# Linear attention and FFN on one core: attention regrouped around (pk x input), 1/den spread by the matmul engine, FFN LayerNorm scale applied after the FFN, two-pass list scheduler

## Chip, cores, metric

One Trainium2 chip, one of its cores. The metric is the device time of one execution in microseconds (us), the median over repeated executions. PE is the matmul engine (TensorE), PEld its weight loads, DVE the vector engine, ACT the scalar (activation) engine, POOL GpSimd, SP the engine that issues the DMAs. "Clock" is the TensorE clock that the throttle granted, as a share of full speed.

## The reference, cut to what matters

Two linear-attention layers and two ReLU FFN layers alternate on one sequence of 2048 tokens and 512 features. There are 32 heads of 16 features, and the FFN is 1376 wide.

```python
def _A_ref(x, wqkv, wo):                       # H = 32, Dh = 16
    q, k, v = qkv[0], qkv[1], qkv[2]           # from x @ wqkv
    phi = lambda t: jnp.where(t > 0, t + 1, jnp.exp(t)) + 1e-6
    pq, pk = phi(q), phi(k)
    kv  = jnp.einsum("bhsd,bhse->bhde", pk, v)
    z   = jnp.einsum("bhsd->bhd", pk)
    num = jnp.einsum("bhqd,bhde->bhqe", pq, kv)
    den = jnp.einsum("bhqd,bhd->bhq", pq, z)[..., None] + 1e-6
    return (num / den) merged over heads @ wo
def _B_ref(x, w1, w2):
    return relu(x @ w1) @ w2

x = A_x
x = x + _A_ref(_layernorm(x), A_wqkv, A_wo)
x = x + _B_ref(_layernorm(x), B_w1, B_w2)
x = x + _A_ref(_layernorm(x), A_wqkv, A_wo)
x = x + _B_ref(_layernorm(x), B_w1, B_w2)
```

(Abridged; the last line of `_A_ref` is put in words.) Every query needs kv and z, which are sums over all tokens. So each attention has a barrier: after the last token's k and v, nothing of num or den can start before kv and z are final.

## The kernel before

The program is a list of operations with their dependences. A list scheduler simulates the engines with a fixed table of costs, emits the order of instructions on each engine and picks the PSUM banks. Tokens are tiles `i` of 128 rows, four tiles are a chunk `t`. The pieces that matter (cuts marked with `...`):

```python
# first half of an attention, per tile: k and v projections, kv accumulated with z as a 129th column
mm_group(... (psv[:, b, :],  Tb[:, i, c, :], wqkv[:, c, D:2*D],   c == 0, c == 3, False) for c in range(4) ...)
mm_group(... (psv[:, b2, :], Tb[:, i, c, :], wqkv[:, c, 2*D:3*D], c == 0, c == 3, False) for c in range(4) ...)
...          # v is evacuated to vext by ACT or DVE; phi(k): 2 operations on ACT, 2 on DVE
mms.append((kv_region(j, KVA, KVB), big[... pk ...], vext[:, i, j, 0:129], st, i == NT - 1, True))

# second half, after the barrier
# a_den: 16 matmuls of 8 columns, then + 1e-6 and a reciprocal on DVE
g.add(DVE, lambda e: e.reciprocal(rden[:, t, :], dene[:, t, :]), ...)
# a_num: 4 matmuls of 128 columns; o = num * (1/den), head by head, on DVE
g.add(DVE, lambda e: e.tensor_tensor(xn[:, i, :]..., psv[:, b, :]..., rden[...].broadcast_to([128, 32, 16]), ALU.mult), ...)
transpose_pe(i)   # chunks 0 to 2: four PE transposes and an evacuation; chunk 3: a transposing DMA
# a_wo: 4 matmuls of 512 columns, then the residual with its row sum, then the sum of squares on ACT
resid(i, b, first_layer, False, True)
ln_next(t)        # mean, variance, pow(-0.5) on POOL, -mean*rstd, normalise, transposing DMA, then the FFN
```

`phi` is evacuated in four operations: ACT x + 1, ACT exp, DVE min, DVE max. The FFN's first matmuls (`b_h`) need the transposed normalised chunk; its second (`b_out`) adds to the residual.

## Time and profile before

| | before |
|---|---|
| time, median of 3 | 308.79 us (308.68 to 308.86) |
| span of the profiled run | 307.2 us |
| PE busy / idle | 295.0 / 12.2 us |
| DVE, ACT busy | 174.7, 178.3 us |
| granted clock | 1.000 |

The first fence is from the profile's page of the kernel before. Its first line gives busy us, share of the span and instructions of each engine. The others cut the span into 40 slices; a digit is the busy share of a slice in tenths. The last line gives the shares of the chain of work that ended last.

```profile
PE 295.0 (96%) x1729; PEld 147.5 (48%) x1755; DVE 174.7 (57%) x486; ACT 178.3 (58%) x359; POOL 18.8 (6%) x29
...
PE   8999999898999999999999999989889999999996
...
DVE  5898867999830381384264556699994026030122
...
PE 81%; DVE 11%; ACT 4%; DMA 3%; issue 1%
```

PE is nearly always busy, and DVE is full over several slices in a row in only two places, 54 to 77 us and 200 to 230 us. These follow the two barriers. The next fence shows PE in the first of them (timeline of PE; start, length, line, operation, output<-inputs, count, and in brackets the idle before and what ended it).

```profile
55.50 0.55 PE L499 MATMUL ps<-Zh,big 128*128 128x8 bf16 x16
55.91 1.05 PE L499 MATMUL ps<-KVbd,big 128*128 128x128 bf16 x16
...
59.05 0.40 PE L465 MATMUL ps<-ident,xn 128*128 128x128 bf16 x4 [1.02 <-DVE xn L612]
...
73.53 3.40 PE L499 MATMUL ps<-wo,Tb 128*128 128x512 bf16 x15 [0.79 <-ACT Tb L469]
77.61 2.76 PE L499 MATMUL ps<-Tb,w 128*128 128x512 bf16 x12 [0.67 <-DMA Tb<-xn]
```

Read lengths with care: a matmul is drawn with its latency (0.38 us for 512 columns), while back-to-back starts give the pitch. Sixteen 8-column matmuls start at 55.50 and the next group at 55.91, which is 26 ns each; 512-column matmuls have a pitch of 0.216 us. The gaps are short and each has another cause: DVE (o = num/den), ACT (evacuation of the transposed o), DMA (transposed input of the FFN). Summed over the kernel, the view of waits of PE gives:

```profile
PE ps L499 <- ACT Tb L469: 2.6, 4, 0.8
PE ps L465 <- DVE xn L612: 2.3, 4, 1.0
PE ps L499 <- DMA Tb<-xn: 1.9, 2, 1.3
PE ps L394 <- DVE wrm L387: 1.2, 1, 1.2
```

### The profile page before, as it was taken

To read this page: it belongs to the slowest core of one execution; us is meant where nothing else is said; L and a number is where in the kernel's file an instruction comes from. 1 tells how busy PE (TensorE), PEld (TensorE's weight loads), DVE (VectorE), ACT (ScalarE), POOL (GpSimd) and SP (SyncE) were. 2 spreads that over 40 slices of the span, in tenths; PEclk is the share of its full clock that TensorE was granted. 3 is DMA by queue.
4 is the path that set the end of the run, shared out by engine and by line. 5 is a ranking of instruction groups with operands and counts; after the bars stand their busy time and mean duration, and the time that the engine had idled before them with its cause. 6 is when DMAs were issued, how large, how long until landed. Compare 5 with 4: busy or idle time off the path is not lost.

```text
span 307.2 us, 4498 instructions
## 1 busy us (share of the span) xinstructions
PE 295.0 (96%) x1729; PEld 147.5 (48%) x1755; DVE 174.7 (57%) x486; ACT 178.3 (58%) x359; POOL 18.8 (6%) x29
## 2 busy tenths in 40 slices
PE   8999999898999999999999999989889999999996
PEld 3455555565444444444544445556534444444444
DVE  5898867999830381384264556699994026030122
ACT  1897857777775385387673357767867605606100
POOL 3211000001200020010000110000111001000000
PEclk9999999999999999999999999999999999999999
DMA  7993400003550016030000033000266002302022
GB/s 229 358 329 70 69 2 0 2 0 67 109 102 0 0 29 109 1 67 3 0 1 2 9 60 68 2 0 2 41 115 121 2 0 68 68 2 68 0 68 70
DMA packets 41765, 17.79 MB, mean 58 GB/s; under 512 B 33584, under 2 KB 41232, under 8 KB 41744
## 3 DMA queue, kind: packets, MB, share of 16 engines
q1 hardware_dynamic: 41744, 17.50, 24.0%
q8 instruction: 14, 0.23, 0.3%
q14 instruction: 7, 0.06, 0.1%
HBM read 7.01 MB, written 2.10 MB: 30 GB/s over the span
## 4 chain that ended last, share of the span: by engine, by line
PE 81%; DVE 11%; ACT 4%; DMA 3%; issue 1%
PE ps L499 78%; DVE xn L612 5%; DMA Tb<-xn 3%; DVE xres L510 2%; PE ps L394 2%; ACT big L479 2%; ACT escr L481 2%; DVE rden L596 2%; DVE xn L444 1%; PE ps L465 1%; DVE big L485 1%; DVE dene L594 0%; DVE emscr L483 0%; ACT Tb L469 0%; DVE xin L652 0%
## 5 line engine op out<-in xcount | busy, mean ns | idle before, releaser
L499 PE MATMUL ps<-Tb,w 128*128 128x512 bf16 (+1 forms) x352 | 77.3, 379 | 1.9 <-DMA Tb<-xn 1.9
L499 PE MATMUL ps<-w,big 128*128 128x512 bf16 (+3 forms) x355 | 76.4, 373 | 0.4
L633 ACT ACTIVATE big<-ps 128x512 bf16<-128x512 f32 (+1 forms) x78 | 46.2, 595 | 29.2 <-PE ps L499 28.8
L499 PE MATMUL ps<-wqkv,Tb 128*128 128x512 bf16 x248 | 58.3, 379 | 1.1 <-ACT Tb L469 0.7
L499 PEld LDWEIGHTS ps<-Tb,w 128*128 128x128 bf16 (+1 forms) x352 | 35.0, 100 | 43.5 <-DMA Tb<-xn 2.9
L499 PEld LDWEIGHTS ps<-w,big 128*128 128x128 bf16 (+1 forms) x363 | 35.3, 97 | 40.6
L516 ACT ACTIVATE sqscr<-xres 128x512 bf16<-128x512 f32 x48 | 30.1, 630 | 41.8 <-DVE xres L510 40.8
L479 ACT ACTIVATE big<-ps 128x512 bf16<-128x512 f32 x64 | 39.2, 613 | 19.1 <-PE ps L499 19.0
L510 DVE SCALAR_TENSOR_TENSOR xres<-ps,xres 128x512 f32<-128x512 f32 x32 | 21.7, 686 | 38.6 <-PE ps L499 38.4
L481 ACT ACTIVATE escr<-ps 128x512 bf16<-128x512 f32 x64 | 39.3, 616 | 0.0
L507 DVE TENSOR_TENSOR xin<-ps,xres 128x512 bf16<-128x512 f32 x15 | 10.4, 692 | 48.8 <-PE ps L499 48.8
L499 PEld LDWEIGHTS ps<-wqkv,Tb 128*128 128x128 bf16 x256 | 24.2, 97 | 26.6 <-ACT Tb L469 0.9
L499 PE MATMUL ps<-wo,Tb 128*128 128x512 bf16 x118 | 28.1, 379 | 2.4 <-ACT Tb L469 1.9
L432 POOL TENSOR_TENSOR rstd<-veps,nhalf 128x4 f32<-128x4 f32 x15 | 15.6, 1041 | 236.6 <-DVE veps L430 218.8
L499 PE MATMUL ps<-Tb,wqkv 128*128 128x512 bf16 x128 | 29.2, 379 | 0.0
L485 DVE TENSOR_TENSOR big<-big,emscr 128x512 bf16<-128x512 bf16 x64 | 26.6, 419 | 1.3
L529 DVE CAST vext<-ps 128x512 bf16<-128x512 f32 x23 | 15.9, 691 | 18.5 <-PE ps L499 18.4
L469 ACT ACTIVATE Tb<-ps 128x512 bf16<-128x512 bf16 x29 | 16.3, 600 | 16.7 <-PE ps L465 16.6
L483 DVE TENSOR_SCALAR emscr<-escr 128x512 bf16<-128x512 bf16 x64 | 18.1, 285 | 5.3 <-ACT escr L481 5.1
L612 DVE TENSOR_TENSOR xn<-ps,rden 128x512 bf16<-128x512 f32 x32 | 20.2, 680 | 0.0
L499 PEld LDWEIGHTS ps<-wo,Tb 128*128 128x128 bf16 x128 | 11.9, 98 | 14.6 <-ACT Tb L469 1.7
L499 PEld LDWEIGHTS ps<-Tb,wqkv 128*128 128x128 bf16 x128 | 12.1, 97 | 12.8
(57 smaller groups left out, 190.0 us busy)
## 6 DMA issues: line engine op xcount, KB each, us to landing
wqkv<-in_A_wqkv_dram SPq DMA_DIRECT2D x3, 512.0 KB, 5.9
xin<-in_A_x_dram SPq DMA_DIRECT2D x3, 512.0 KB, 8.7
out_dram<-xin SPq DMA_DIRECT2D x3, 512.0 KB, 2.9
w<-in_B_w_dram SPq DMA_DIRECT2D x1, 1376.0 KB, 11.0
w<-in_B_w_dram SPq DMA_DIRECT2D x1, 1280.0 KB, 13.8
wo<-in_A_wo_dram SPq DMA_DIRECT2D x1, 512.0 KB, 8.8
xin<-in_A_x_dram SPq DMA_DIRECT2D x1, 384.0 KB, 3.2
Tb<-xn SPq DMA_TRANSPOSE x16, 4.3
```

The source lines that it names most:

```text
L432: g.add(POOL, lambda e: e.tensor_tensor(rstd[:, sl], veps[:, sl], nhalf[:, 0:4], ALU.pow), [("veps", t), ("nhalf",)], [("rstd", t)], C_POO ...
L469: g.add_flex([(ACT, lambda e: e.activation(dst, psb()[:, :], ACTF.Identity), C_ACT_PSUM), (DVE, lambda e: e.tensor_copy(dst, psb()[:, :]), ...
L479: g.add(ACT, lambda e: e.activation(dst_ap, psv[:, b, :], ACTF.Identity, bias=1.0 + 1e-6, scale=1.0), [("ps", b)], [dst_key], C_ACT_PSUM, ...
L481: g.add(ACT, lambda e: e.activation(escr[:, s, :], psv[:, b, :], ACTF.Exp), [("ps", b)], [("escr", s)], C_ACT_EXP, name=name + "_exp")
L483: g.add(DVE, lambda e: e.tensor_scalar(emscr[:, s, :], escr[:, s, :], 1.0, 1e-6, ALU.min, ALU.add), [("escr", s)], [("emscr", s)], C_DVE_B ...
L485: g.add(DVE, lambda e: e.tensor_tensor(dst_ap, dst_ap, emscr[:, s, :], ALU.max), [dst_key, ("emscr", s)], [dst_key], 340.0, name=name + "_ ...
L499: last = e.matmul(o, l, r, start=st, stop=sp, skip_group_check=skip)
L510: g.add(DVE, lambda e: e.scalar_tensor_tensor(xres[:, i, :], psv[:, b, :], 0.0, src, ALU.add, ALU.add, accum_out=s1[:, i:i + 1]), [("ps", ...
L516: g.add(ACT, lambda e: e.activation(sqscr[:, q, :], xres[:, i, :], ACTF.Square, accum_out=s2[:, i:i + 1]), [("xres", i)], [("sqscr", q), ( ...
L529: (DVE, lambda e: e.tensor_copy(vext[:, i, :, 0:128], psv[:, b2, :].rearrange("p (j f) -> p j f", f=128)), C_DVE_FLEX)],
L612: g.add(DVE, lambda e: e.tensor_tensor(xn[:, i, :].rearrange("p (h f) -> p h f", f=16), psv[:, b, :].rearrange("p (h f) -> p h f", f=16), ...
L633: g.add_flex([(ACT, lambda e, M=M, b=b, u=u: e.activation(unit_ap(u, M), psv[0:M, b, :], ACTF.Relu), C_ACT_PSUM), (DVE, lambda e, M=M, b=b ...
```

## The change

The intent: let PE do less. `num/den @ wo` is regrouped.

- **(pk x input) instead of v.** kv = pk^T (xn Wv) = (pk^T xn) Wv. So G = xn^T pk is summed over all tokens in four PSUM banks; after the barrier one small product with Wv gives kv transposed, and `wo` is folded into it: Wp = kv wo. v is never made, nor o, nor the transposes of o.
- **1/den by PE.** den comes as 32 rows (8 heads, each four times) per head group, from four 32-column matmuls packed side by side in the array. ACT takes exp(-ln(den)); DVE splits it into a bf16 high and low part; four packed 32-row matmuls with a 0/1 matrix spread it over the features and add the two parts. DVE then multiplies pq, and the `wo` matmuls read pq/den directly.
- **FFN scale moved.** ReLU is positively homogeneous, so the FFN gets x - mean only, and rstd multiplies its output in the residual operation.
- **Scheduler.** A backward pass gives each operation the length of the work that follows it as priority, a forward pass builds the schedule, six rounds, the best kept. Before it was one forward pass that took the earliest start within a window.
- Smaller things: two-tile transposing DMAs instead of four-tile ones, another order of loads, the first chunk's LayerNorm tile by tile, the activation table that holds Ln and Exp.

The core of the diff (cuts marked `...`):

```diff
-            b2 = alloc_bank()
-            mm_group(... Tb[:, i, c, :], wqkv[:, c, 2 * D:3 * D] ...  "vproj%d" % i)
...
+            mm_group(lambda: [(psv[:, GB[c], :], xn[:, i, 128 * c:128 * c + 128], big[:, u * 512:u * 512 + 512],
+                               i == 0, i == NT - 1, False) for c in range(4)], ... "gacc%d" % i)
...
+                mm_group(lambda b=b, j=j: [(psv[:, b, :], KVT[:, j, :], wo[:, j, :], True, True, False)], ... "wp%d" % j)
...
-            g.add(DVE, lambda e: e.reciprocal(rden[:, t, :], dene[:, t, :]), ...
+            mm_group(lambda: [(psv[32 * j:32 * j + 32, b, :], Zc[:, j, :], unit_ap(us[j]), True, True, False) for j in range(4)], ...
+            g.add(ACT, lambda e: e.activation(lden[:, s, :], psv[:, b, :], ACTF.Ln, bias=eps6[:, 0:1]), ...
+            g.add(ACT, lambda e: e.activation(lden[:, s, :], lden[:, s, :], ACTF.Exp, scale=-1.0), ...
+            g.add(DVE, lambda e: e.tensor_copy(rhi[:, s, :], lden[:, s, :]), ...
+            g.add(DVE, lambda e: e.scalar_tensor_tensor(rsp[:, s, :], rhi[:, s, :], rneg[:, 0:1], lden[:, s, :], ALU.mult, ALU.add), ...
+            mm_group(lambda: [(psv[:, GB[j], :], esel[32 * j:32 * j + 32, :], rsp[32 * j:32 * j + 32, s, :], True, True, False)
+                              for j in range(4)], ...
+                g.add(DVE, lambda e, j=j: e.tensor_tensor(unit_ap(us[j]), unit_ap(us[j]), psv[:, GB[j], :], ALU.mult), ...
...
-            resid(i, b, first_layer, False, True)
+            resid_a(i, b, first_layer)          # residual, row sum, then xn = x - mean
-            resid(i, b, False, last_layer, not last_layer)
+            resid_f(i, b, last_layer)           # x + rstd * (FFN output)
...
-def _list_schedule(ops, tile_ops, vbank, nbanks=8):
+def _backward(ops, succ, rank):
+def _forward(ops, succ, tile_ops, nbanks, fixed_sp):
+def _list_schedule(ops, tile_ops, vbank, fixed_sp, iters=6, nbanks=8):
```

## The prediction

> **What bounds it now.** The profile's page gives PE 295.0 us busy of a 307.2 us span (96%), ACT 58%, DVE 57%, granted clock 1.0; the chain that ended last is 81% PE. So the time is PE's issue stream plus 12 us of PE idle. The timeline of PE gives the pitch of back-to-back matmuls: 512 columns 216 ns, 129-column kv accumulation 58, 128-column numerator and transposes 56, 8-column denominator 26, warm-up 410. Counts times pitch: 1216 x 0.216 = 262.7 (attention 512, FFN 704), kv 7.4, numerator 7.2, transposes 7.2, denominator 3.3, warm-up 6.6; sum 294.4, which closes on 295.0. The idle (windows, timeline): start about 2, end 2.65, and per attention about 3.5 to 4 between the last q projection and the first FFN matmuls, where DVE is over 99% busy (60 to 70 us) and PE waits on DVE's normalisation, ACT evacuation and the transposing DMA.
>
> **PE ledger of the change.**
> - Out: v projection 128 x 0.216 = 27.6 us, kv accumulation 7.4, numerator 7.2, denominator 3.3, 112 of 128 transposes 6.3. Sum 51.8.
> - In: pk x input, 128 matmuls of 512 columns, 27.6: it only replaces the v projection. z with one column, 128 x 26 ns = 3.3; kvT 32 x 56 ns = 1.8; folding wo 8 x 0.216 = 1.7; den and 1/den broadcast, 64 tiled 512-column matmuls in 16 groups of four. The Trainium skill ("TensorE: Matmul & The Clock Gate", "Measured speedup vs the span model") states 3.07x for four row tiles of K=32, N=512; an estimate of 0.28 us a group from that gives 4.5 us (no run shows it yet; unpacked 13.8). Sum 38.9.
> - Net -13: PE about 281.5.
>
> **Other engines.** ACT and DVE lose 32 v evacuations (0.6 us each), 24 o-transpose evacuations, 8 reciprocals (0.95); they gain 16 evacuations of G and Wp, and per chunk Ln, Exp and hi/lo split (about 2.2 us). The 32 PSUM multiplies of 0.6 stay, on pq instead of o. The FFN scale moved past the FFN takes variance, POOL pow (1.04 us) and nbias out of the path from residual to FFN transpose. All off the PE bound, but the den chain (about 2.5 us plus 2.4 us of multiplies) must be covered by q, Wp and other matmuls; the emitted order puts about 2.6 us there. DVE just after the barrier (about 18 us against 15 us of PE by my count) is still tight.
>
> **Idle after.** Start 3 to 4 (first useful matmul waits for two tiles; chunk 1 waits for a transposing DMA behind the loads), end 2.7, per attention 2 to 2.5: 11 to 12 us, about as now. The rescheduling I credit with at most 2 us.
>
> Span 281.5 + 11.5 = 293; the time ran 1.6 us over the span: **294.5 us**, range **289.5 to 301**. Chances: faster by over 2% 0.90, within 2% 0.08, slower 0.02.
>
> **What would show it.** PE busy near 281; groups of four tiled matmuls spaced near 0.28 us (0.86: no packing, time near 303); 512-column pitch still 216 ns; PE idle before the first FFN matmuls of each attention 1 to 2.5 us; one activation-table load; no new wait over 2 us on the transposing DMA at 15 to 25 us.
>
> **What would make it wrong.** Tiles not overlapping or draining PE on each mode switch (+3 to +9 us); DVE overload after the barrier (+2 to +5); early transposes held behind loads (+2 to +4); better overlap than I credit (idle 7 us, time near 290); a lower granted clock.

## The result

| | before | after |
|---|---|---|
| time, same rounds, median of 4 | 308.74 us (308.54 to 308.86) | 295.04 us (294.85 to 295.59) |
| ratio after / before | | 0.9563 (95%: 0.9549 to 0.9576) |
| span of the profiled run | 307.2 | 293.0 |
| PE busy / idle | 295.0 / 12.2 | 282.9 / 10.1 |
| DVE, ACT busy | 174.7, 178.3 | 164.0, 171.8 |
| granted clock | 1.000 | 1.000 |

A ratio is the mean time of one kernel's fast runs over that of the other's of the same rounds, so it is not quite the ratio of the medians beside it. "Idle" is always the span less the busy time of PE on the page.

The same lines of the page, after:

```profile
PE 282.9 (97%) x1470; PEld 129.3 (44%) x1491; DVE 164.0 (56%) x485; ACT 171.8 (59%) x349; POOL 20.7 (7%) x32
...
PE   7999999989999999999999999998999999999996
...
DVE  5998637996349551480326474599832955130233
...
PE 83%; DVE 11%; DMA 3%; issue 1%; SPq 0%
```

PE lost 12.1 us of work and 2.1 us of idle, and that is the whole 14.2 us of span. Of the 12.1 us, 1.4 are no merit of the change: the 16 warm-up matmuls ahead of the first real one took 6.6 us before and 5.2 after. In both traces they first start 0.427 us apart and then 0.216; the switch comes after the 15th in one and after the 8th in the other. The timeline of PE after the first barrier:

```profile
45.58 1.05 PE L573 MATMUL ps<-GT,wqkv 128*128 128x128 bf16 x16
46.57 0.40 PE L573 MATMUL ps<-big,Zc 128*32 128x512 bf16 x4
46.90 1.04 PE L573 MATMUL ps<-Tb,wqkv 128*128 128x512 bf16 x4
...
53.90 3.62 PE L573 MATMUL ps<-Wp,big 128*128 128x512 bf16 x16
57.44 0.40 PE L573 MATMUL ps<-rsp,esel 32*128 32x512 bf16 x4
57.77 2.76 PE L573 MATMUL ps<-Tb,wqkv 128*128 128x512 bf16 x12
60.47 0.40 PE L573 MATMUL ps<-big,Zc 128*32 128x512 bf16 x4
62.29 2.54 PE L573 MATMUL ps<-Wp,big 128*128 128x512 bf16 x11 [1.43 <-DVE emscr L557]
```

A packed group of four takes 0.33 us from its start to the next (46.57 to 46.90, 57.44 to 57.77). There is a little more ahead of it: 0.09 us in the trace, from the start of the matmul before the group, with one pitch taken off. One long wait is left, 1.43 us, and it comes again in the second attention. The view names DVE L557, a min of phi(q) that the `wo` matmuls do not read; the weight loads of PE wait for DVE big L720, the multiply by 1/den (3.8 us in four waits). Either way it is DVE. These are the two longest entries in the view of waits of PE:

```profile
PE ps L573 <- DVE emscr L557: 2.9, 2, 1.4
PE ps L464 <- DVE wrm L457: 1.2, 1, 1.2
```

The total came as forecast. The profile alone would suggest the account that the forecast gave: PE does 12 us less, so the kernel is 13.7 us faster. The experiments show that this is true as bookkeeping of the two end states and wrong as an account of causes.

### The profile page after: what moved, and what is told of

Its sections match the earlier page's. It is cut to its first block, busy times and chain, and to the rows that moved or that the text cites. A ratio compares the mean times of both kernels' runs of the same rounds, so it can differ in the third digit from the quotient of the medians.

```text
span 293.0 us, 4025 instructions
## 1 busy us (share of the span) xinstructions
PE 282.9 (97%) x1470; PEld 129.3 (44%) x1491; DVE 164.0 (56%) x485; ACT 171.8 (59%) x349; POOL 20.7 (7%) x32
## 4 chain that ended last, share of the span: by engine, by line
PE 83%; DVE 11%; DMA 3%; issue 1%; SPq 0%
PE ps L573 83%; DVE big L720 3%; DMA xin<-in_A_x_dram 2%; DVE xres L586 2%; DMA Tb<-xn 1%; DVE big L559 1%; DVE Wp L652 1%; DVE bst L483 1%; DVE emscr L557 1%; DVE xn L593 1%; DVE rsp L714 1%; DVE rhi L713 0%; DVE xn L515 0%; DVE nmf L589 0%; DVE xin L760 0%
## 5 line engine op out<-in xcount | busy, mean ns | idle before, releaser
L741 ACT ACTIVATE big<-ps 128x512 bf16<-128x512 f32 (+1 forms) x81 | 48.2, 596 | 29.4 <-PE ps L573 28.9
L613 DVE SCALAR_TENSOR_TENSOR xin<-ps,rstdf,xres 128x512 bf16<-128x512 f32 x15 | 11.3, 750 | 38.5 <-PE ps L573 38.5
L573 PE MATMUL ps<-wqkv,Tb 128*128 128x512 bf16 x125 | 31.4, 379 | 0.3
L573 PE MATMUL ps<-Wp,big 128*128 128x512 bf16 x124 | 28.7, 379 | 3.0 <-DVE emscr L557 2.9
L573 PE MATMUL ps<-big,xn 128*128 128x512 bf16 x124 | 31.3, 379 | 0.2
L557 DVE TENSOR_SCALAR emscr<-escr 128x512 bf16<-128x512 bf16 x64 | 17.8, 290 | 21.7 <-ACT escr L555 21.2
L617 DVE SCALAR_TENSOR_TENSOR xres<-ps,rstdf,xres 128x512 f32<-128x512 f32 x16 | 12.0, 751 | 24.8 <-PE ps L573 24.8
L720 DVE TENSOR_TENSOR big<-big,ps 128x512 bf16<-128x512 bf16 x32 | 20.1, 681 | 7.9 <-PE ps L573 7.9
L573 PEld LDWEIGHTS ps<-Wp,big 128*128 128x128 bf16 x128 | 12.2, 98 | 17.6 <-DVE big L720 3.0
L573 PEld LDWEIGHTS ps<-big,xn 128*128 128x128 bf16 x128 | 12.5, 98 | 15.1 <-DVE big L559 0.2
L573 PEld LDWEIGHTS ps<-wqkv,Tb 128*128 128x128 bf16 x128 | 12.2, 98 | 15.2 <-DMA Tb<-xn 0.6
L606 POOL TENSOR_TENSOR rstdf<-varf,nhalf 128x4 f32<-128x4 f32 x8 | 8.1, 1007 | 144.6 <-DVE varf L604 144.6
```

The source lines that it names most:

```text
L557: g.add(DVE, lambda e: e.tensor_scalar(emscr[:, s, :], escr[:, s, :], 1.0, 1e-6, ALU.min, ALU.add), [("escr", s)], [("emscr", s)], C_DVE_B ...
L573: last = e.matmul(o, l, r, start=st, stop=sp, skip_group_check=skip)
L606: g.add(POOL, lambda e: e.tensor_tensor(rstdf[:, sl], varf[:, sl], nhalf[:, 0:4], ALU.pow), [("varf", t), ("nhalf",)], [("rstdf", t)], C_P ...
L613: g.add(DVE, lambda e: e.scalar_tensor_tensor(xin[:, i, :], psv[:, b, :], rstdf[:, i:i + 1], xres[:, i, :], ALU.mult, ALU.add), rd, [("xin ...
L617: g.add(DVE, lambda e: e.scalar_tensor_tensor(xres[:, i, :], psv[:, b, :], rstdf[:, i:i + 1], xres[:, i, :], ALU.mult, ALU.add, accum_out= ...
L720: g.add(DVE, lambda e, j=j: e.tensor_tensor(unit_ap(us[j]), unit_ap(us[j]), psv[:, GB[j], :], ALU.mult), [("big", us[j]), ("ps", GB[j])], ...
```

## The experiments

The theory at the start was the forecast's: the shorter matmul stream of the new attention makes the gain, and order and scale move matter little. The rival was that order and scale move make it. All variants gave correct results. Times are medians; the kernel before had medians of 308.5 to 308.8 us. Runs 9 and 10 were made on another chip than runs 1 to 8. The edits are shown abridged.

### 1. The kernel before with the new scheduler alone

```diff
-def _list_schedule(ops, tile_ops, vbank, nbanks=8):        # one pass, windows
+# _succs, _backward, _forward, _list_schedule of the kernel after, unchanged
+# with its table of costs (issuing a DMA 470 instead of 60 ns)
```

> The kernel before with nothing changed but the two-pass scheduler. Theory (the gain is a shorter matmul stream): the stream keeps its 294.4 us, only the idle time can shrink; 306 to 309 us, PE busy 294 to 296. Rival (the gain is mainly the better order of instructions): at least half of the 13.7 us gain appears here, 302 us or less, with PE idle falling from 12 to about 5 us.

Measured: 304.22 us, ratio 0.9827 (0.9784 to 0.9869). PE busy 293.3, idle 9.2. It fell between the two expectations: about a third of the gain (4.5 us), with the same operations. PE idle in the stretches around the two barriers (50 to 80 and 200 to 230 us) fell from 6.5 to 2.4 us. The forecast's "at most 2 us" for the order was too small already here.

### 2. The kernel after with the old scheduler

```diff
-# two-pass _list_schedule
+# one-pass _list_schedule of before (the order of loads and first transposes, and the table of costs, as in after)
```

> The kernel after with the old one-pass list scheduler (the order of the loads and first transposes kept as in after). Theory: 295 to 300 us, PE busy 281 to 284, any loss is PE idle around the barrier. Rival (the order makes the gain): 302 us or more.

Measured: 306.29 us, ratio 0.9887 (0.9835 to 0.994). The theory's range was missed by 6 us and the rival's was met: nearly the whole gain is gone, though PE has the same matmuls to do. As the table of costs stayed, the table alone does not make the gain. Idle is 17.4 us and PE busy 287.9 us, 5.0 more than after (the profiled run was the slowest of its four, 307.19 us). About half of the idle is waits on DVE; the two longest:

```profile
PE ps L517 <- DVE nmf L533: 4.6, 2, 2.6
PE ps L517 <- DVE big L664: 2.5, 1, 2.5
```

Of the 5.0 us of busy time, 1.1 are longer warm-ups. The timeline of PE around the first barrier says where more of it comes from:

```profile
54.57 0.38 PE L517 MATMUL ps<-wo,KVT 128*128 128x512 bf16 x1 [0.16 <-issue]
55.14 0.39 PE L517 MATMUL ps<-wo,KVT 128*128 128x512 bf16 x1 [0.19 <-ACT escr L499]
56.12 0.39 PE L517 MATMUL ps<-wo,KVT 128*128 128x512 bf16 x1 [0.59 <-ACT escr L499]
56.61 0.89 PE L517 MATMUL ps<-big,Zc 128*32 128x512 bf16 x8
58.08 5.25 PE L517 MATMUL ps<-Wp,big 128*128 128x512 bf16 x16 [0.58 <-ACT Wp L595]
```

The 16 `wo` matmuls take 5.25 us where the kernel after takes 3.62 for the same group. Three windows of the same trace (stretch; its length; busy us and count of PE, PEld, DVE, ACT, POOL; granted clock; DMA share; GB/s):

```profile
54.00:58.00 4.00, 2.37 (x16) 0.61 (x16) 3.96 (x11) 4.00 (x10) 0.00 (x0) 1.00 0.00 0
58.00:62.00 4.00, 3.92 (x11) 1.49 (x12) 2.11 (x8) 3.46 (x8) 0.00 (x0) 0.57 0.02 4
57.99:61.40 3.41, 3.32 (x8) 1.20 (x9) 1.76 (x7) 2.87 (x8) 0.00 (x0) 0.50 0.02 5
```

PE was idle for 41% of the first window (2.37 us busy of 4.00), in gaps none of which was longer than 0.59 us, and in the next window the granted clock was 0.57. That is an average: the clock was 0.50 for 3.41 us and 1.00 before and after. So idle here cost twice: once as waiting, once as slow matmuls after it. The Trainium skill ("TensorE: Matmul & The Clock Gate", section "What's actually happening") describes a clock gate that halves the PE clock after an idle activity window of about 3.4 us; the trace agrees in the half clock and in the 3.41 us that it lasted. The skill's section "Why this matters for your kernels" asks for no idle gaps above about 3 us; here the clock fell after gaps of 0.59 us and less. What sets it off is not shown, and the share of idle alone does not decide it: in run 3 PE was busy for only 1.31 of the 3.41 us from 61.31 to 64.72, and the clock stayed at 1.00 until 71.55.

### 3. The kernel after with the FFN scale back in front of the FFN

```diff
-            ... nmf = -mean; xn = xres + nmf                      # centring only
-                        tr_chunk(t - WO_LAG, TGF); ln_ffn(t - WO_LAG)
+                        ln_next(t - WO_LAG)      # mean, variance, pow, nbias, normalise, transpose
-   x + rstd * (FFN output)
+   x + (FFN output)
```

> The kernel after with the LayerNorm scale put back in front of the FFN (variance, pow and nbias again between the residual and the FFN transpose; no centring op). Theory: the latency is covered by other matmuls; 294.5 to 297 us, PE busy unchanged at 283. Rival (moving the scale removed the waits before the FFN that before showed, 3.5 to 4 us per attention): 299 us or more, with PE idle before the first FFN matmuls of each attention up by 2 us or more.

Measured: 305.14 us, ratio 0.9856 (0.9796 to 0.9916). Again the theory missed and the rival was met: +10 us against after. PE busy 284.4, idle 18.5. The view of waits, its two longest, and the timeline of PE after the first barrier:

```profile
PE ps L573 <- DMA Tb<-xn: 5.1, 3, 2.5
PE ps L573 <- DVE veps L501: 4.2, 2, 2.1
```

```profile
63.41 3.40 PE L573 MATMUL ps<-Wp,big 128*128 128x512 bf16 x15 [2.10 <-DVE veps L501]
66.74 0.39 PE L573 MATMUL ps<-rsp,esel 32*128 32x512 bf16 x4
68.43 0.40 PE L573 MATMUL ps<-big,Zc 128*32 128x512 bf16 x4 [1.29 <-DVE big L559]
71.18 14.16 PE L573 MATMUL ps<-Tb,w 128*128 128x512 bf16 x57 [2.35 <-DMA Tb<-xn]
```

The first FFN matmul starts at 71.18 us; in the kernel after it starts at 64.66. The late q projections are used up by then, so PE has nothing else. The latency that the forecast called covered is on the critical path once the attention's own PE work is short. Two things are not separated here. The edit also changes the grain: the scaled normalisation needs the statistics of four tiles, x - mean is made tile by tile. And of the 5.7 us of gaps shown, 3.4 are waits on DVE and 2.4 on the transposing DMA.

### 4. den and the broadcast of 1/den unpacked

```diff
-  (psv[32*j:32*j+32, b, :], Zc[:, j, :],  pq_j, True, True)          # four side by side
+  (psv[:, b, :],            Zf[:, j, :],  pq_j, j == 0, j == 3)      # zero-padded to 128 columns
-  (psv[:, GB[j], :], esel[32*j:32*j+32, :], rsp[32*j:32*j+32, s, :])
+  (psv[:, GB[j], :], eself[:, j, :],        rsp[:, s, :])            # zero-padded to 128 rows
```

> The kernel after with den and the broadcast of 1/den as full 128-row, 128-column matmuls on zero-padded weights instead of four packed tiles; same result. A group of four should take 4 x 0.216 = 0.86 us instead of 0.33 us, 16 groups: +8.5 us of PE. Theory (PE's stream bounds the time, also around the barrier): 302 to 304.5 us. Rival (around the barrier DVE bounds, so PE time there is partly free): 300 us or less, with the PE waits of 1.4 us before the wo matmuls shrinking.

Measured: 298.68 us, ratio 0.9649 (0.9607 to 0.9691). The theory's range (302 to 304.5) was missed; the rival's was met. PE busy rose by 6.8 us to 289.7, but idle fell from 10.1 to 7.4 us. Of the 6.8 us, 0.2 are longer warm-ups. The wait before the `wo` matmuls is gone from its timeline:

```profile
59.56 2.75 PE L577 MATMUL ps<-Tb,wqkv 128*128 128x512 bf16 x12
62.15 1.03 PE L577 MATMUL ps<-big,Zf 128*128 128x512 bf16 x4
63.01 3.62 PE L577 MATMUL ps<-Wp,big 128*128 128x512 bf16 x15
66.96 9.67 PE L577 MATMUL ps<-Tb,w 128*128 128x512 bf16 x44 [0.34 <-DMA Tb<-xn]
```

So after the barrier PE time is partly free: PE either works or waits for the other engines. Two numbers follow. An unpacked group takes 0.86 us (62.15 to 63.01). And 6.8 us over 16 groups is 0.43 us a group, so a packed group costs about 0.86 - 0.43 = 0.43 us of PE in all. The trace of after gives the same: 0.33 seen from start to start and 0.09 ahead of it, 0.42. The Trainium skill ("TensorEngine Tiling (Array Packing)", "Key Properties") says that changing the tiling mode drains the engine; the gaps of 0.09 us ahead of the groups agree with that, and run 10, where two den groups stand back to back, shows how much of the 0.42 us is such a change.

### 5. The v projection kept

```diff
-  G accumulation (4 x 512 columns a tile), evacuation of G, kvT
+  v projection (4 x 512 columns a tile), its evacuation, kv^T accumulated with 4 x 128 columns a tile
```

> The kernel after with the v projection and a kv accumulation of 128-column matmuls kept in place of pk x input and kvT; all else (folded wo, packed den, order, FFN scale) as in after. PE ledger per attention: +64 x 0.216 +64 x 0.056 -64 x 0.216 -16 x 0.056 = +2.7 us, so PE busy about 288. Theory (pk x input is only an exchange, it saves the small kv matmuls): 299 to 302 us. Rival (the exchange costs a serial tail after the last token: evacuation of G, kvT; keeping v hides it): 296 us or less with less PE idle around the barrier.

Measured: 299.12 us, ratio 0.9665 (0.9614 to 0.9717). The theory held. PE busy 288.7, 5.8 above after (forecast from the ledger: 5.4; 0.8 of the 5.8 are longer warm-ups). Idle is 8.5, 1.6 less than after, as the rival said, but far from enough. (pk x input) saves no large matmul; it saves the small kv matmuls and the v evacuations, 4.1 us of time together. (Wv is also loaded earlier in this run, as it is needed sooner.)

### 6. 1/den in one bf16

```diff
-  ACT: lden = exp(-lden) in f32;  DVE: rhi = bf16(lden);  DVE: rsp = lden - rhi on the low rows
+  ACT: rsp = exp(-lden) straight in bf16           # esel picks one row per head instead of two
```

> The kernel after with 1/den in one bf16 instead of a hi and a lo half: Exp writes bf16 straight from ACT, the copy (0.42 us) and the subtraction (0.75 us) on DVE go, 8 times each. Theory (the 1.43 us wait of PE before the second group of wo matmuls is DVE's backlog after the barrier): that wait falls below 0.5 us, PE idle by 2 to 3 us, 292 to 293.5 us. Rival (the wait is latency of ACT or PSUM banks): 294.5 us or more. Should be correct within the tolerance; if not, the time still counts.

Measured: 292.26 us (291.68 to 293.25), ratio 0.9444 (0.9409 to 0.948), correct. PE busy is unchanged at 282.9 and idle is 7.4 us, 2.7 less (0.8 of that in the first 10 us, where the warm-ups were 1.4 us longer). The wait at the barrier was halved, not quite as far as expected:

```profile
PE ps L573 <- DVE emscr L557: 1.6, 2, 0.8
```

The removed operations are DVE's alone, and PE's idle shrank: the wait before the second group of `wo` matmuls is DVE's. That it is a backlog and not the length of the chain shows in the timeline of DVE in after: no idle from 51.65 to 62.3 us, and the four multiplies start at 59.53, 1.7 us after the broadcast matmuls ended (57.84). This variant beats both kernels.

### 7. The kernel before with the new scheduler and the scale move

```diff
+# scheduler as in 1, and resid_a / ln_ffn / resid_f of the kernel after; attention as before
```

> The kernel before with the two-pass scheduler and the FFN scale moved past the FFN, attention as before. Theory (the attention rewrite alone shortens PE's stream, the other two only remove idle, of which the scheduler alone left about 9 us, 5 of them start and end): PE busy 292 to 295, 301 to 304 us. Rival (the parts simply add, and the scale move is worth the 10 us that putting it back cost): 296 us or less.

Measured: 300.93 us, ratio 0.9727 (0.9683 to 0.9771). It is a hair below the theory's range and far from the rival's. PE busy 292.5, idle 6.6. These two parts give 7.9 us without touching the attention: idle falls by 5.6 us, and of the 2.5 us less PE busy 1.2 are shorter warm-ups.

### 8. The attention rewrite alone

```diff
+# as 3 (scale in front of the FFN), and with the one-pass scheduler as in 2
```

> The attention rewrite alone: old one-pass scheduler, FFN scale in front of the FFN. Theory (it shortens the stream by 12 us but takes away the matmuls that filled PE around the barrier, and idle PE also loses its clock): 306 to 313 us, little or no gain, idle 18 us or more, granted clock below 1 after the barrier. Rival (its 12 us of PE show in full): 299 us or less.

Measured: 310.15 us, ratio 1.0039 (0.9974 to 1.0104): no gain. The second theory, formed after runs 1 to 4, held. From its page and its view of waits:

```profile
PE 284.7 (93%) x1469; PEld 129.6 (42%) x1491; DVE 164.5 (53%) x469; ACT 174.8 (57%) x349; POOL 20.4 (7%) x32
```

```profile
PE ps L517 <- DVE big L645: 8.5, 4, 3.1
PE ps L517 <- ACT escr L499: 2.5, 4, 1.2
PE ps L483 <- DVE xn L459: 2.2, 2, 1.2
```

PE's work did fall by 10.3 us, and its idle rose by 10.6 us to 22.8. The clock averaged 0.994 (0.83 in the stretch from 60 to 70 us). The two traces show where the saved work went: in the first attention the sums over tokens (G and z here, kv with z before) are done at 46.56 us here and at 50.49 in the kernel before, yet the first FFN matmul starts at 77.42 here and at 77.61 there (225.15 and 224.85 in the second attention). What the shorter stream won ahead of the barrier was lost after it, mostly waiting for DVE, which was busy for 28.9 of the 30 us from 200 to 230. One rival stays untested: the order in which the program lists the operations, and the window of the old scheduler, were not tuned again for the new attention.

### 9. The scale move alone

```diff
+# resid_a / ln_ffn / resid_f of the kernel after in the kernel before, nothing else
```

> The kernel before with nothing changed but the FFN scale moved past the FFN (old scheduler, old attention). It completes the table of the three parts. Theory (PE's stream is unchanged; at most the waits in front of the first FFN matmuls, 1.9 us on the transposing DMA and part of 2.6 us on the Tb evacuation, can go): 304 to 308 us. Rival (the scale move alone is worth what putting it back cost after, 10 us): 300 us or less.

Measured: 307.39 us, ratio 0.9972 (0.9942 to 1.0003). The theory held: almost nothing, and the interval holds 1. PE busy 294.8, idle 10.8.

### 10. Single bf16, den of two chunks first

```diff
-  DEN_PRE=1, LATE_A=1
+  DEN_PRE=2, LATE_A=0
```

> The single-bf16 variant with den of two chunks emitted right after the barrier, ahead of all late q projections. Theory (what is left at the barrier is DVE's backlog): 290.5 to 292.5 us, at best 1.6 us less than the single-bf16 variant, whose two waits of 0.78 us there are all that is left to win. Rival (the earlier den makes DVE's work bunch up): 293 us or more.

Measured: 291.47 us (291.01 to 291.71), ratio 0.9442 (0.9428 to 0.9457). It met the range, but against the kernel before it stands exactly where run 6 stands (0.9444), so it isn't shown to be better. The barrier waits on DVE fell from 1.6 to 0.4 us in all, while the first 10 us had 3.3 us of PE idle against 1.7. Idle is 7.8 us.

This order also puts two packed den groups back to back (timeline of PE):

```profile
46.88 0.61 PE L573 MATMUL ps<-big,Zc 128*32 128x512 bf16 x8
47.43 1.04 PE L573 MATMUL ps<-Tb,wqkv 128*128 128x512 bf16 x4
```

Two groups take 0.55 us from start to start where one took 0.33, so the second adds only 0.22 us, with no gap ahead of it. Of the 0.42 us that a lone den group costs, about 0.20 is going into the packed mode and out of it again: 0.09 ahead and 0.11 behind. Groups placed next to each other share that cost.

### The three parts together

The eight combinations of scheduler (S), scale move (L) and attention rewrite (A). Span, busy and idle are of one profiled run each; busy includes the warm-ups (6.6, 5.9, 6.2, 5.4, 5.5, 6.4, 6.3 and 5.2 us from top to bottom). The rows come from several calls, so differences of about 1 us between rows should not be read:

| parts | time | span | PE busy | PE idle |
|---|---|---|---|---|
| none | 308.79 | 307.2 | 295.0 | 12.2 |
| L | 307.39 | 305.6 | 294.8 | 10.8 |
| S | 304.22 | 302.5 | 293.3 | 9.2 |
| S + L | 300.93 | 299.1 | 292.5 | 6.6 |
| A | 310.15 | 307.5 | 284.7 | 22.8 |
| A + L | 306.29 | 305.3 | 287.9 | 17.4 |
| A + S | 305.14 | 302.9 | 284.4 | 18.5 |
| A + S + L | 295.04 | 293.0 | 282.9 | 10.1 |

Read the two halves. Without A, the idle goes from 12.2 to 6.6 us. With A it goes from 22.8 to 10.1 us, of which S alone recovers 4.3 and L alone 5.4 us. A gains nothing on "none" (+1.4 us, its interval holds 1), nothing that can be told from noise on S (+0.9) or on L (-1.1), and 5.9 us on S + L. In that last step PE busy falls by 9.6 us and idle grows by 3.5 us, some of which run 6 takes back.

## Why the prediction was right, point by point

- **Time and its terms: right.** 294.5 us was forecast, 295.04 measured; PE busy 281.5 forecast, 282.9 measured; idle 11.5 forecast, 10.1 measured. The 512-column pitch stayed 0.216 us. Counting the matmuls and multiplying by pitches read from the trace of before was enough for the end state. That the span came out at 293.0 to the tenth is luck: busy was 1.4 us too low and idle 1.4 us too high. Without the warm-ups PE busy fell by 10.7 us where the ledger says 12.9, and the packed groups explain about that difference.
- **(pk x input) only replaces v: right.** Run 5: +5.8 us of PE busy (5.0 without the warm-ups) where 5.4 was computed.
- **Packed groups at 0.28 us: mis-sized.** They took 0.33 us from start to start and about 0.43 us in all (run 4), which makes 16 groups 6.9 us instead of 4.5. What the forecast left out of the sum is the change of mode, about 0.20 us a group (run 10, for the den groups); it had named that among the things that could go wrong, at 3 us or more in all. The skill's 3.07x for row tiles ("TensorE: Matmul & The Clock Gate", "Measured speedup vs the span model") would be 0.86/0.28; here, in a stream of other matmuls, it was 0.86/0.43 = 2.0. They do overlap: the fear of 0.86 us was wrong.
- **"Net -13: PE about 281.5" as the cause of the gain: wrong step.** The fall in PE work is real with A alone (run 8, -10.3 us), and the time did not fall. What the sum missed is that PE's stream is not the limit between the barrier and the FFN: with A alone and the old order, the sums over tokens ended 3.9 us earlier and the first FFN matmul only 0.2 us earlier, in the second attention not at all.
- **"The rescheduling I credit with at most 2 us": wrong.** Alone it gave 4.5 us (run 1); taken out of the finished kernel it costs 11.3 us (run 2).
- **"All off the PE bound", said of the other engines' changes with the scale move among them: wrong.** Putting the scale back costs 10.1 us (run 3). By itself in the old kernel it gives about 1 us, not clear of noise (run 9), and with the new scheduler but the old attention 3.3 us (runs 1 and 7): its worth grows as less other work is left to hide it.
- **"DVE just after the barrier is still tight": right**, and the wait of 1.43 us per attention lies inside the 2 to 2.5 us of idle forecast there. Run 6 shows that it is DVE's.
- **One activation-table load, no new wait over 2 us on the early transposes: right.** The profile has one table load, and its view of waits of PE names none on the transposing DMA.

Why was the total right with two causes mis-sized? The idle after was estimated from the emitted order of the finished kernel, which already held the scheduler's and the scale move's work. So the end state was counted correctly; only the shares were not.

Left open: the smaller parts (two-tile transposes, order of loads, first LayerNorm tile by tile) were not separated; they are in all runs with A and in none without. Nor was it tested what makes up the 1.6 to 3.3 us of idle in the first 10 us, which differs between kernels with nearly the same start. The warm-ups in it took 5.0 us (run 10) to 6.6 us (before, run 6); the traces show that this is how long PE starts a matmul every 0.427 us before it goes over to 0.216, but not what sets that moment.

## What to carry to other kernels

When a change removes work from the busiest engine, ask at which moment that work ran: here, work taken out after a barrier, where another engine was full, gave nothing until order and latency there were mended too. Bookkeeping of busy and idle predicts the end state well but does not say which part of a change earned it; take each part out of the finished kernel and put each alone into the old one before dropping any as unneeded. After a barrier shorten the chain first (fewer operations on the engine with the backlog, latency moved behind the next big matmuls), then cut matmuls, and keep the gaps from piling up, as PE may lose its clock on top.

## What the Trainium skill lacked or had wrong

- "TensorE: Matmul & The Clock Gate", "Back-to-back issue gap": it states a sustained 131 ns per matmul for 512 columns and 81 ns for 128, and calls its own formula (216 and 56 ns) an over- and an undercount. Here load-and-multiply pairs ran at 216 ns for 512 columns in long streams and at 56 ns for 128 columns in groups of 16, so the formula fits and the roofline figures don't.
- The same page, "Why this matters for your kernels": the rule of no idle gap above about 3 us is not enough. In run 2 gaps of at most 0.59 us, 41% idle over 4 us, were followed by a granted clock of 0.50 for 3.41 us, while in run 3 62% idle over 3.41 us (61.31 to 64.72) was not. (The page's section "A second HAM failure mode: psum-queue depth-cycling" mentions micro-idles without a size.)
- The same page, "Measured speedup vs the span model": 3.07x for a group of four packed tiles. Between full-size matmuls a group cost 0.43 us against 0.86 us unpacked, 2.0x; the page doesn't count the cost of entering and leaving the packed mode. "TensorEngine Tiling (Array Packing)" names the drain but gives no size; here it was 0.09 us ahead of a group and, for groups of four 32-column tiles, 0.11 us behind (run 10). The second of two such groups in a row took 0.22 us.
